# Scatters of token rows in pairs, gathered rows at another address, and the first expert's transposes spread between the last gate products

## The chip, the cores and the metric

One core of one Trainium2 chip runs the whole program. The metric is device time in microseconds (us), from the host's view of one execution; a profiled execution also has a span, from its first to its last instruction. Its engines work side by side and meet through semaphores: TensorE (PE, with PEld for its weight loads), VectorE (DVE), ScalarE (ACT), GpSimd (POOL) and SyncE (SP, which only starts transfers here).

## What is computed

Attention over q and k whose pairs count only where six sign bits of a projection agree, then a mixture of eight experts with two experts for each token, then a dense layer with a sigmoid gate. Cut from the reference:

```python
q_bits = (np.einsum('bhsd,dk->bhsk', q, proj) > 0)           # 2 x 8 heads x 768 x 64
mask = q_bucket[:, :, :, None] == k_bucket[:, :, None, :]
scores = np.where(mask, scale * q @ k.T, -1e9)
x = softmax(scores) @ v                                       # 1536 tokens x 512
noisy_logits = x @ w_gate + np.log1p(np.exp(x @ w_noise)) * noise
top2, top2_w = ...                                            # two experts of eight, softmax of the two
for e in range(8):
    out[mask] += top2_w * (np.maximum(x[mask] @ w1[e], 0) @ w2[e])
h = out @ w_in
return (h / (1 + np.exp(-1.702 * h))) @ w_out
```

## The kernel before

The 1536 tokens are four blocks `bq` of 384 (batch and half of the sequence), each of three row blocks of 128. The attention stage is one loop over `g` from -3 to 95 (L660 and on). A step holds the scores of one head's 128 queries against 768 keys two steps ahead (`a_score(g + 2)`, PE L320), their row maximum and the two scalars that the exponential wants (`a_soft`, DVE L332 to L334, tile `sm`), the transposes of the exponentials of step `g` (`a_trans`, PE L360, six of 128x128, whose copies out of PSUM go to ACT L289 or DVE L295), the exponential itself (ACT L343), every second step the product with the values (`a_av`, PE L370), and then the extra jobs that a table written by hand (`sched`) gives to that step. Tile then keeps the program's order on each engine; nothing is reordered.

Among the extra jobs are the hash and the operands of the heads to come (`a_hash`, PE L185; `a_hb`, DVE L200; `a_split` and `a_sub`, whose last part is a POOL subtraction, L219), gate products (`a_xt`, L410, with the DVE lines L403 to L417), routing (`r_do`), loads and splits of expert weights (`w_load`; `w_conv`, POOL L912), and the scatters. `r_scatter(bq, i)` sends row block `i` of `bq` to its two experts' row lists in HBM: two indirect DMAs issued by POOL (L513), each of 128 rows of 2 KB, and before each a one-element memset of a tile `spacer` (L512). On POOL they stand in trains: (0,0) and (0,1) are four scatters, (0,2) is two, bq 1 is six, bq 2 six, and bq 3 six in the expert stage.

After the loop comes the handover to the experts. The last two gate products `a_xt(15, 1)` and `a_xt(15, 2)` run; `f_tr` turns the first expert's rows (loaded as `xrow0`, three row blocks, 320 rows) by four PE transposes a block (L818) into `xeh`, copied by ACT (L819), with the remainders `xel` by a DVE subtraction (L820). PSUM banks of pool `ps_s` take two blocks and of `ps_p` one. Then the first expert's product (`f_s1`, PE L1048, 320 columns), the routing of bq 3 between its parts, and its rank products (PE L480) that need the table M (DVE L472).

At the other end, before the dense layer, `p_gather(t)` fetches each token's two expert results `yg` by indirect DMAs on POOL (L1268); `p_comb` weighs and adds them (ACT, DVE L1281 into `x`), and PE transposes the sum (L1295). The pool for this stage (`p_pools`) is laid over memory of the expert stage, in order of first use: `yg` comes first and lies where `xol` lay, which DVE L919 reads for its last split.

Of the kernel before, what the change touches and what calls it, by code (L numbers as in the profile page):

```python
# [9 lines left out]
F32 = mybir.dt.float32  # L10
# [4 lines left out]
AF = mybir.ActivationFunctionType  # L15
ALU = mybir.AluOpType
# [6 lines left out]
DM = 512  # L23
# [7 lines left out]
CAPA = 320  # L31
# [9 lines left out]
class Kernel:  # L41
# [282 lines left out]
    def a_soft(self, g):  # L324
        nc = self.nc
        u, s, n, qh, j, c = self.dec(g)
        ps = self.S.pop(g)
        if s == 0:
            self.RS[u] = self.rsum[u % 4]
        mx = self.t(self.ap, [128, 1], F32, "mx", 4)  # L330
        sm = self.t(self.ap, [128, 2], F32, "sm", 4)
        nc.vector.tensor_reduce(mx, ps[:, :, :HALF], axis=AX.XY, op=ALU.max, negate=True)  # L332
        nc.vector.tensor_scalar(sm[:, 0:1], mx, BIG / 2, None, op0=ALU.is_lt)
        nc.vector.tensor_scalar(sm[:, 1:2], mx, BIG / 2, mx, op0=ALU.is_lt, op1=ALU.mult)  # L334
        self.sm[g] = (sm, ps)
        self.use(dve=1.15)

    def a_exp(self, g):
# [170 lines left out]
    def r_scatter(self, bq, i):  # L509
        nc = self.nc  # L510
        for k in range(2):
            nc.gpsimd.memset(self.spacer, 0.0)  # L512
            st = nc.gpsimd.indirect_dma_start(  # L513
                out=self.xs, out_offset=bass.IndirectOffsetOnAxis(ap=self.slot[:, bq * 3 + i, k:k + 1], axis=0),
                in_=self.XR[bq][:, i, :], in_offset=None)
            for o in self.scat:
                self.tc.declare_no_dep(st.ins, o.ins, reason="every token has its own slot")
            self.scat.append(st)
# [15 lines left out]
    def attention(self):  # L534
# [3 lines left out]
        nc = self.nc  # L538
# [8 lines left out]
        for g, *f in (  # L547
# [158 lines left out]
            (56, self.w_load, 5),  # L706
            (56, self.r_do, 1, "soft"),
            (57, self.r_do, 1, "noisy", "top"),
            (57, self.r_scatter, 0, 1),
            (58, self.r_do, 1, "index"),  # L710
            (58, self.r_do, 0, "weights"),
            (59, self.w_conv, 4),
            (59, self.a_hash, 6),
# [19 lines left out]
            (67, self.r_scatter, 1, 0),  # L733
            (68, self.a_loadv, 6),
            (68, self.a_hash, 7),
            (69, self.r_scatter, 1, 1),
            (70, self.r_scatter, 1, 2),
            (70, self.a_hb, 7, 0),
            (70, self.a_uv, 7),
            (70, self.a_split, 7, 0, 0),  # L740
# [5 lines left out]
            (72, self.a_sub, 7, 1, 0, "p"),  # L746
            (73, self.a_xt, 11),
            (73, self.w_load, 6),
            (73, self.a_split, 7, 1, 1),
            (73, self.a_sub, 7, 1, 1, "p"),  # L750
            (75, self.w_load, 7),
# [31 lines left out]
            self.la, self.ld = max(self.la, 2.1 * g), max(self.ld, 2.1 * g)  # L783
        self.attn = False
        self.a_av(15, 2)
        self.a_xt(15, 1)
        self.a_xt(15, 2, True)
        self.f_tr()
        self.r_stage(3, 0, 3)
        self.r_do(3, "soft")  # L790
        self.f_s1(0)
# [15 lines left out]
            self.nc.sync.dma_start(t[:, i, :], x[i * 128:(i + 1) * 128, :])  # L807
        self.xrow[0] = t

    def f_tr(self):  # L810

        nc = self.nc
        xh, xl = self.xT[0] = self.x_tiles(0)
        for i, (o, w) in enumerate(self.tiles(0)):
            pt = self.t(self.ps_p, [128, 512], F32, "p") if i == 2 else self.t(self.ps_s, [128, 2, 512], F32, "s")[:, 0, :]
            pt = pt.rearrange("p (d n) -> p d n", d=4)
            for d in range(4):
                nc.tensor.transpose(pt[:, d, :], self.xrow[0][:, i, d * 128:(d + 1) * 128], self.ident)  # L818
            nc.scalar.activation(xh[:, :, o:o + w], pt[:, :, :w], AF.Copy)  # L819
            nc.vector.tensor_tensor(xl[:, :, o:o + w], pt[:, :, :w], xh[:, :, o:o + w].bitcast(F32), op=ALU.subtract)  # L820

    def f_s1(self, f):
        nc = self.nc
        ps = self.t(self.ps_s, [128, 2, 512], F32, "s")[:, 0, :CAPA]
        self.m_mm1(0, f, ps)
        if f >= 3:
            self.m_h(0, f, ps)
            return
        hh, hl = self.hT[0]
        h = self.t(self.ap, [128, CAPA], F32, "P", 3)  # L830
        nc.scalar.activation(h, ps, AF.Relu)
        nc.scalar.activation(hh[:, f, :], h, AF.Copy)
        nc.gpsimd.tensor_tensor(hl[:, f, :], h, hh[:, f, :].bitcast(F32), op=ALU.subtract)
# [421 lines left out]
    def p_pools(self, ctx):  # L1255
        self.pp = self.pool("mlp", ctx=ctx, side="right")
        self.ps_g = self.pool("ps_g", 2, PSUM, ctx=ctx)
        self.ps_o = self.pool("ps_o", 4, PSUM, ctx=ctx)
        self.ps_u = self.pool("ps_u", 2, PSUM, ctx=ctx)
        self.maxload = NU + 16  # L1260
        self.x2T, self.gT, self.op, self.yg, self.x2 = {}, {}, {}, {}, {}

    def p_gather(self, t):
        nc = self.nc
        ys = []
        for k in range(2):
            y = self.t(self.pp, [128, DM], F32, f"yg{k}", 2)
            st = nc.gpsimd.indirect_dma_start(  # L1268
                out=y, out_offset=None, in_=self.ys,
                in_offset=bass.IndirectOffsetOnAxis(ap=self.ysl[:, t, k:k + 1], axis=0))  # L1270
            ys.append(y)
            if t < 6:
                self.early.append(st)
        self.yg[t] = ys
# [331 lines left out]
```

## Time and profile before

| | us |
|---|---|
| median of 3 runs | 863.45 (861.52, 863.50, 863.45) |
| the profiled execution | 861.88 |
| its span | 860.2 |
| PE busy in the span | 838.9 (98%) |
| DVE, ACT, POOL busy | 524.7, 434.4, 222.8 |
| mean granted TensorE clock | 0.994 |

The profile gives for each engine its busy time, for each instruction when it began, how long it ran and how long its engine stood idle ahead of it (with what ended that). A row in square brackets below names an engine's idle time and the instruction that ended it. The granted clock is 1.00 at TensorE's full 2.4 GHz and 0.50 at its lower level of 1.2 GHz.

### The profile page before, as it was taken

Reading aid. Unit: us, or ns where it says so; the run is one execution under the profiler, and the core shown is the slowest. Engines: PE = TensorE matmul, PEld = TensorE weight load, DVE = VectorE, ACT = ScalarE, POOL = GpSimd, SP = SyncE. Lnnn points to the kernel's source line nnn. Section 1 sums busy time; section 2 is a strip of 40 time slices with the busy share of each in tenths; the row PEclk is TensorE's granted clock in tenths of the full one; section 3 lists DMA queues with packets and bytes.
Section 4 is the critical chain, followed back from the end, with each engine's and each line's share of the span. In section 5 each row is a group of like instructions: output and inputs, shape, how many; then the busy total and the mean of one; then the engine's idle time right before and its main releaser. Section 6 shows DMA issues by size and latency. Waiting matters only on the chain.

```text
span 860.2 us, 15512 instructions
## 1 busy us (share of the span) xinstructions
PE 838.9 (98%) x6104; PEld 775.6 (90%) x6104; DVE 524.7 (61%) x1068; ACT 434.4 (51%) x772; POOL 222.8 (26%) x235
## 2 busy tenths in 40 slices
PE   8999999889989999999999999998999999999997
PEld 6888888769979999999999999988899998989897
DVE  7787878667764698989889898747622121312120
ACT  6887988757763544454545353556623131414140
POOL 4531746474024000000000000007614151504040
PEclk9999999999999999999999999999999999999999
DMA  7646845441135577877879686738301010010000
GB/s 253 215 151 217 237 139 162 148 135 45 38 112 208 199 250 245 293 238 258 280 247 291 207 288 207 239 111 317 124 26 50 25 42 33 27 49 2 25 1 28
DMA packets 49854, 132.47 MB, mean 154 GB/s; under 512 B 6256, under 2 KB 8496, under 8 KB 49776
## 3 DMA queue, kind: packets, MB, share of 16 engines
q1 hardware_dynamic: 41280, 109.38, 38.5%
q0 software_dynamic: 6960, 20.37, 7.7%
q10 hardware_dynamic: 1536, 1.67, 0.6%
q8 instruction: 50, 0.82, 0.4%
q14 instruction: 28, 0.23, 0.1%
HBM read 92.23 MB, written 35.39 MB: 148 GB/s over the span
## 4 chain that ended last, share of the span: by engine, by line
PE 93%; DMA 2%; DVE 2%; another core or an unknown queue 1%; issue 1%; ACT 1%; ACTq 0%; POOL 0%; DVEq 0%; POOLq 0%; SPq 0%
PE g L1318 15%; PE h L1048 15%; PE s L320 8%; PE av L370 8%; PE p L360 7%; PE y L1070 5%; PE y L1072 5%; PE y L1071 5%; PE o L1365 4%; PE o L1363 4%; PE o L1364 4%; PE s L1048 2%; PE t L1089 2%; DMA rawk<-in_kT 1%; PE t L1025 1%; PE m L410 1%
## 5 line engine op out<-in xcount | busy, mean ns | idle before, releaser
L332 DVE TENSOR_REDUCE mx<-s 128x1 f32<-128x768 f32 x96 | 91.6, 954 | 31.8 <-PE s L320 25.3
L1327 POOL TENSOR_TENSOR gl<-sg,gh 128x512 fp32r<-128x512 f32 x48 | 66.1, 1376 | 157.6 <-ACT gh L1326 157.6
L343 ACT ACTIVATE P<-s,sm 128x768 f32<-128x768 f32 x96 | 95.3, 993 | 22.3 <-DVE sm L334 20.2
L1268 POOL DMA_INDIRECT yg<-ys,cst x24 | 25.5, 1062 | 303.2 <-DVE wl L919 296.8
L320 PE MATMUL s<-v,u 76*128 76x384 f32 (+1 forms) x384 | 93.3, 364 | 0.4 <-ACT P L343 0.2
L1323 DVE TENSOR_TENSOR sg<-g,sg 128x512 f32<-128x512 f32 x48 | 33.2, 692 | 93.6 <-ACT sg L1322 91.7
L360 PE MATMUL p<-cst,P 128*128 128x128 f32 x576 | 80.3, 275 | 9.2 <-ACT hh L289 4.5
L360 PEld LDWEIGHTS p<-cst,P 128*128 128x128 f32 x576 | 68.8, 141 | 15.0 <-ACT hh L289 5.8
L320 PEld LDWEIGHTS s<-v,u 76*128 76x128 f32 (+1 forms) x384 | 63.4, 191 | 13.7 <-issue 9.0
L1053 ACT ACTIVATE hh<-h 128x416 fp32r<-128x416 f32 x56 | 29.1, 519 | 72.9 <-PE h L1048 72.4
L1070 PE MATMUL y<-hh,wh 128*128 128x416 f32 (+1 forms) x144 | 51.1, 355 | 0.0
L1322 ACT ACTIVATE sg<-g 128x512 f32<-128x512 f32 x48 | 28.7, 599 | 42.2 <-PE g L1318 38.0
L1072 PE MATMUL y<-hh,wl 128*128 128x416 f32 (+1 forms) x144 | 49.8, 346 | 0.0
L1071 PE MATMUL y<-hl,wh 128*128 128x416 f32 (+1 forms) x144 | 49.8, 346 | 0.0
L1326 ACT ACTIVATE gh<-sg 128x512 fp32r<-128x512 f32 x48 | 30.3, 631 | 31.7 <-DVE sg L1323 30.9
L1054 DVE SCALAR_TENSOR_TENSOR hl<-h,hh 128x416 fp32r<-128x416 f32 x56 | 32.9, 588 | 14.4 <-ACT hh L1053 14.2
L289 ACT ACTIVATE hh<-p 128x384 f32<-128x384 f32 x71 | 31.7, 487 | 17.1 <-PE p L360 7.8
L1318 PE MATMUL g<-bth,wh 128*128 128x256 f32 x144 | 39.9, 277 | 0.0
L1318 PE MATMUL g<-x2h,wh 128*128 128x256 f32 x144 | 39.9, 278 | 0.0
L1318 PE MATMUL g<-btl,wh 128*128 128x256 f32 x144 | 39.8, 276 | 0.0
L1318 PE MATMUL g<-bth,wl 128*128 128x256 f32 x144 | 39.8, 276 | 0.0
L1318 PE MATMUL g<-x2h,wl 128*128 128x256 f32 x144 | 39.7, 277 | 0.0
(328 smaller groups left out, 2489.4 us busy)
## 6 DMA issues: line engine op xcount, KB each, us to landing
ws<-in_w SPq DMA_DIRECT2D x40, 512.0 KB, 5.8
d_in<-in_w SPq DMA_DIRECT2D x32, 512.0 KB, 5.3
bth<-in_w SPq DMA_DIRECT2D x16, 512.0 KB, 4.6
btl<-in_w SPq DMA_DIRECT2D x16, 512.0 KB, 4.9
wd<-d_o SPq DMA_DIRECT2D x32, 256.0 KB, 3.8
xs<-xeh SPq DMA_DIRECT2D x13, 512.0 KB, 6.0
rawq<-in_qT SPq DMA_DIRECT2D x14, 384.0 KB, 5.3
rawk<-in_kT SPq DMA_DIRECT2D x14, 384.0 KB, 4.7
```

Source lines behind the costliest of these rows:

```text
L320: nc.tensor.matmul(ps[:, hf, :HALF], l[:kk, q0:q0 + 128], r[:kk, hf * HALF:(hf + 1) * HALF], start=st, stop=not st)
L332: nc.vector.tensor_reduce(mx, ps[:, :, :HALF], axis=AX.XY, op=ALU.max, negate=True)
L343: nc.scalar.activation(P, ps[:, :, :HALF], AF.Exp, bias=sm[:, 1:2], scale=sm[:, 0:1], accum_out=self.RS[u][:, c, j, 0:1])
L360: nc.tensor.transpose(ps[:, kb, :], P[:, hf, kb * 128:(kb + 1) * 128], self.ident)
L370: nc.tensor.matmul(self.pa[64 * j:64 * j + 64, c * 128:(c + 1) * 128], self.vt[n][:, kb, 64 * j:64 * j + 64], PT[:, j, kb, :], start=(kb = ...
L1048: nc.tensor.matmul(ps, self.units[8 * e + d][w][:, fs], y[:, d, :n], start=(i == 0), stop=(i == 11))
L1070: nc.tensor.matmul(ps, wh[:, ds_], hh[:, f, :], start=(f == 0), stop=False)
L1071: nc.tensor.matmul(ps, wh[:, ds_], hl[:, f, :], start=False, stop=False)
L1072: nc.tensor.matmul(ps, wl[:, ds_], hh[:, f, :], start=False, stop=(f == 7))
L1318: nc.tensor.matmul(ps[:, x, :], self.units[NU + 4 * (f // 8) + d][w][:, fs], y[:, d, :], start=(i == 0), stop=(i == 11))
L1327: nc.gpsimd.tensor_tensor(gl[:, fo, :], g, gh[:, fo, :].bitcast(F32), op=ALU.subtract)
L1363: nc.tensor.matmul(ps, gh[:, f, o], wh[:, ws], start=(f == 0), stop=False)
```

## The change

Three edits:

1. The scatters of bq 0 and 1. Ahead of the first of each pair, the spacer is no longer a memset but a POOL copy from the newest `sm` tile, kept in `self.smt`: POOL waits until DVE has written the scalars of score `g + 2`. The second keeps its memset. In the table, (0,1) moves from step 57 to 58, (1,1) from 69 to 70, and (1,2) from 70 to 73. (0,0), (0,2) and (1,0) keep their steps.
2. `f_tr` becomes `f_hi` (a block's PE transposes and ACT copy) and `f_lo` (its DVE remainder). The blocks stand before `a_xt(15, 1)` and between it and `a_xt(15, 2)`; their banks are now one of `ps_s`, one of `ps_p` and the product's own `pa`; the first product of the expert goes to the bank of the gate products (`mt`).
3. `p_pools` reserves four buffers (`sg` and `x2`, two each) ahead of all others, so that `yg` comes 8 KB a partition further on, over `yT` and `yrow`.

```diff
@@ -333,6 +333,7 @@
         nc.vector.tensor_scalar(sm[:, 0:1], mx, BIG / 2, None, op0=ALU.is_lt)
         nc.vector.tensor_scalar(sm[:, 1:2], mx, BIG / 2, mx, op0=ALU.is_lt, op1=ALU.mult)
         self.sm[g] = (sm, ps)
+        self.smt = sm
         self.use(dve=1.15)
 
     def a_exp(self, g):
@@ -509,7 +510,10 @@
     def r_scatter(self, bq, i):
         nc = self.nc
         for k in range(2):
-            nc.gpsimd.memset(self.spacer, 0.0)
+            if bq < 2 and k == 0:
+                nc.gpsimd.tensor_copy(self.spacer, self.smt[0:1, 0:1])
+            else:
+                nc.gpsimd.memset(self.spacer, 0.0)
             st = nc.gpsimd.indirect_dma_start(
                 out=self.xs, out_offset=bass.IndirectOffsetOnAxis(ap=self.slot[:, bq * 3 + i, k:k + 1], axis=0),
                 in_=self.XR[bq][:, i, :], in_offset=None)
@@ -706,8 +710,8 @@
             (56, self.w_load, 5),
             (56, self.r_do, 1, "soft"),
             (57, self.r_do, 1, "noisy", "top"),
-            (57, self.r_scatter, 0, 1),
             (58, self.r_do, 1, "index"),
+            (58, self.r_scatter, 0, 1),
             (58, self.r_do, 0, "weights"),
             (59, self.w_conv, 4),
             (59, self.a_hash, 6),
@@ -733,8 +737,7 @@
             (67, self.r_scatter, 1, 0),
             (68, self.a_loadv, 6),
             (68, self.a_hash, 7),
-            (69, self.r_scatter, 1, 1),
-            (70, self.r_scatter, 1, 2),
+            (70, self.r_scatter, 1, 1),
             (70, self.a_hb, 7, 0),
             (70, self.a_uv, 7),
             (70, self.a_split, 7, 0, 0),
@@ -746,6 +749,7 @@
             (72, self.a_sub, 7, 1, 0, "p"),
             (73, self.a_xt, 11),
             (73, self.w_load, 6),
+            (73, self.r_scatter, 1, 2),
             (73, self.a_split, 7, 1, 1),
             (73, self.a_sub, 7, 1, 1, "p"),
             (75, self.w_load, 7),
@@ -783,9 +787,13 @@
             self.la, self.ld = max(self.la, 2.1 * g), max(self.ld, 2.1 * g)
         self.attn = False
         self.a_av(15, 2)
+        self.f_hi(0)
         self.a_xt(15, 1)
+        self.f_hi(1)
+        self.f_hi(2)
+        for i in range(3):
+            self.f_lo(i)
         self.a_xt(15, 2, True)
-        self.f_tr()
         self.r_stage(3, 0, 3)
         self.r_do(3, "soft")
         self.f_s1(0)
@@ -807,21 +815,28 @@
             self.nc.sync.dma_start(t[:, i, :], x[i * 128:(i + 1) * 128, :])
         self.xrow[0] = t
 
-    def f_tr(self):
-
-        nc = self.nc
-        xh, xl = self.xT[0] = self.x_tiles(0)
-        for i, (o, w) in enumerate(self.tiles(0)):
-            pt = self.t(self.ps_p, [128, 512], F32, "p") if i == 2 else self.t(self.ps_s, [128, 2, 512], F32, "s")[:, 0, :]
-            pt = pt.rearrange("p (d n) -> p d n", d=4)
-            for d in range(4):
-                nc.tensor.transpose(pt[:, d, :], self.xrow[0][:, i, d * 128:(d + 1) * 128], self.ident)
-            nc.scalar.activation(xh[:, :, o:o + w], pt[:, :, :w], AF.Copy)
-            nc.vector.tensor_tensor(xl[:, :, o:o + w], pt[:, :, :w], xh[:, :, o:o + w].bitcast(F32), op=ALU.subtract)
+    def f_hi(self, i):
+        nc = self.nc
+        if i == 0:
+            self.xT[0] = self.x_tiles(0)
+            self.xps = []
+        o, w = self.tiles(0)[i]
+        pt = (self.t(self.ps_s, [128, 2, 512], F32, "s")[:, 0, :] if i == 0 else self.t(self.ps_p, [128, 512], F32, "p") if i == 1
+              else self.pa)
+        pt = pt.rearrange("p (d n) -> p d n", d=4)
+        for d in range(4):
+            nc.tensor.transpose(pt[:, d, :], self.xrow[0][:, i, d * 128:(d + 1) * 128], self.ident)
+        nc.scalar.activation(self.xT[0][0][:, :, o:o + w], pt[:, :, :w], AF.Copy)
+        self.xps.append(pt)
+
+    def f_lo(self, i):
+        o, w = self.tiles(0)[i]
+        xh, xl = self.xT[0]
+        self.nc.vector.tensor_tensor(xl[:, :, o:o + w], self.xps[i][:, :, :w], xh[:, :, o:o + w].bitcast(F32), op=ALU.subtract)
 
     def f_s1(self, f):
         nc = self.nc
-        ps = self.t(self.ps_s, [128, 2, 512], F32, "s")[:, 0, :CAPA]
+        ps = self.t(self.ps_s, [128, 2, 512], F32, "s")[:, 0, :CAPA] if f else self.mt([128, CAPA])
         self.m_mm1(0, f, ps)
         if f >= 3:
             self.m_h(0, f, ps)
@@ -1259,6 +1274,10 @@
         self.ps_u = self.pool("ps_u", 2, PSUM, ctx=ctx)
         self.maxload = NU + 16
         self.x2T, self.gT, self.op, self.yg, self.x2 = {}, {}, {}, {}, {}
+        for _ in range(2):
+            self.t(self.pp, [128, 2, self.CH], F32, "sg", 2)
+        for _ in range(2):
+            self.t(self.pp, [128, DM], F32, "x2", 2)
 
     def p_gather(self, t):
         nc = self.nc
```

On POOL, from the last weight split ahead of bq 1's scatters to their end (`wl` is that split; `xel` holds bq 1's rows; `u_8`, `v_8` are the last head's operands). Before:

```order
L912 TENSOR_TENSOR wl_2751<-ws_2359,wh_2750 128x1024
L512 MEMSET spacer_138 1x1
L513 DMA xs<-xel_761,slot_137 15360x512
...
L170 DMA u_8_2906<-u_8_2905 64x768
...
L219 TENSOR_TENSOR v_8_2910<-rawk_8_2268,v_8_2909 64x768
L219 TENSOR_TENSOR u_8_2907<-rawq_8_2270,u_8_2907 64x768
L219 TENSOR_TENSOR v_8_2912<-rawk_8_2272,v_8_2911 64x768
```

After:

```order
L927 TENSOR_TENSOR wl_2751<-ws_2359,wh_2750 128x1024
L514 COPY spacer_138<-sm_2760 1x1
L517 DMA xs<-xel_761,slot_137 15360x512
...
L514 COPY spacer_138<-sm_2867 1x1
...
L170 DMA u_8_2902<-u_8_2901 64x768
...
L219 TENSOR_TENSOR u_8_2903<-rawq_8_2270,u_8_2903 64x768
L514 COPY spacer_138<-sm_2986 1x1
...
L219 TENSOR_TENSOR v_8_2908<-rawk_8_2272,v_8_2907 64x768
```

Where six scatters stood in a row behind the weight split, there are two pairs now, the second behind a copy of its own, and the third pair stands between the last two subtractions of the head's operands.

On PE, from the last product with the values to the first expert's first product (`xrow` are the expert's rows, `xu` the attention rows of the last two gate products). Before:

```order
L370 MATMUL av_96<-hl_3695,v_3173 64x128 x12
L410 MATMUL m_3753<-cst_124,xu_3718 128x160
L410 MATMUL p_3761<-cst_124,xu_3751 128x160
L818 MATMUL s_3771<-cst_124,xrow_1_3624 128x128 x4
L818 MATMUL s_3778<-cst_124,xrow_1_3624 128x128 x4
L818 MATMUL p_3785<-cst_124,xrow_1_3624 128x128 x4
L1048 MATMUL s_3806<-xeh_3769,wh_1412 128x320
```

After:

```order
L371 MATMUL av_96<-hl_3695,v_3173 64x128 x12
L828 MATMUL s_3755<-cst_124,xrow_1_3624 128x128 x4
L411 MATMUL m_3761<-cst_124,xu_3718 128x160
L828 MATMUL p_3769<-cst_124,xrow_1_3624 128x128 x4
L828 MATMUL av_96<-cst_124,xrow_1_3624 128x128 x4
L411 MATMUL p_3783<-cst_124,xu_3751 128x160
L1063 MATMUL m_3805<-xeh_3753,wh_1412 128x320
```

The first block's transposes now stand ahead of both gate products, the others between them. On DVE the three `xel` subtractions accordingly stand ahead of the last gate product's lines instead of behind them.

## Rows read from the trace of the kernel before

**Rows 1.** Waits of PE over the whole span: us in total, times, longest.

```profile
PE p L360 <- ACT hh L289: 4.5, 3, 2.5
PE u L1295 <- DVE x L1281: 2.3, 2, 1.5
```

**Rows 2.** Windows: length; busy PE, PEld, DVE, ACT, POOL; granted clock, DMA share, GB/s.

```profile
124.78:134.36 9.58, 9.58 (x105) 8.12 (x104) 8.42 (x30) 7.01 (x17) 0.00 (x0) 1.00 0.16 59
149.36:163.84 14.48, 11.96 (x106) 9.65 (x105) 8.98 (x38) 8.23 (x19) 4.28 (x7) 0.88 0.43 167
168.54:178.19 9.65, 9.65 (x96) 8.79 (x95) 7.76 (x27) 9.11 (x20) 9.07 (x12) 1.00 0.58 154
183.38:200.13 16.75, 12.49 (x105) 9.80 (x104) 8.47 (x19) 6.79 (x13) 10.53 (x19) 0.80 0.46 146
241.00:257.00 16.00, 12.79 (x127) 10.75 (x126) 9.72 (x34) 9.25 (x21) 6.33 (x11) 1.00 0.41 149
192.00:195.00 3.00, 2.48 (x14) 1.75 (x16) 2.01 (x5) 2.13 (x4) 0.00 (x0) 0.50 0.23 87
```

**Rows 3.** POOL's scatters in the timeline: start, us, instruction, idle before it.

```profile
149.45 1.09 POOL L513 DMA_INDIRECT xs<-xr,slot  x1 [0.18 <-DVE xeh L417]
153.41 0.97 POOL L513 DMA_INDIRECT xs<-xr,slot  x1 [0.22 <-issue]
...
172.16 1.05 POOL L513 DMA_INDIRECT xs<-xr,slot  x1 [0.17 <-POOL spacer L512]
...
184.23 1.02 POOL L513 DMA_INDIRECT xs<-xel,slot  x1 [0.16 <-issue]
...
190.66 0.97 POOL L513 DMA_INDIRECT xs<-xel,slot  x1 [0.21 <-issue]
```

**Rows 4.** PE and DVE at the first stall of each of the two trains, timeline.

```profile
153.73 0.96 DVE L332 TENSOR_REDUCE mx<-s 128x1 f32<-128x768 f32 x1 [2.21 <-PE s L320]
155.67 0.93 PE L360 MATMUL p<-cst,P 128*128 128x128 f32 x6 [2.52 <-ACT hh L289]
188.46 0.68 DVE L200 TENSOR_SCALAR hb<-p,hdr 128x384 fp32r<-128x384 f32 x1 [2.94 <-PE p L360]
189.19 0.55 PE L360 MATMUL p<-cst,P 128*128 128x128 f32 x3 [2.23 <-issue]
```

**Rows 5.** POOL's last subtractions and PE's scores behind them, timeline.

```profile
196.54 0.56 POOL L170 DMA_DIRECT2D u<-u  x1 [4.91 <-ACT u L169]
207.11 1.82 POOL L219 TENSOR_TENSOR v<-rawk,v 64x768 fp32r<-64x768 f32 x1
211.18 0.97 PE L320 MATMUL s<-v,u 128*128 128x384 f32 x4
```

**Rows 6.** The handover to the first expert, timeline of ACT, PE and DVE.

```profile
259.54 0.28 ACT L289 ACTIVATE xu<-av 128x128 f32<-128x128 f32 x1 [1.61 <-PE av L370]
260.88 1.08 ACT L819 ACTIVATE xeh<-s 128x512 fp32r<-128x512 f32 x2 [1.06 <-PE s L818]
261.86 0.39 ACT L819 ACTIVATE xeh<-p 128x256 fp32r<-128x256 f32 x1
262.95 0.38 PE L1048 MATMUL s<-xeh,wh 128*128 128x320 f32 x1 [1.23 <-DVE xel L820]
266.98 0.21 DVE L472 TENSOR_REDUCE M<-oh 128x24 bf16<-128x48 f32 x1
268.29 0.18 PE L480 MATMUL m<-M,tri 128*128 128x8 bf16 x1
```

**Rows 7.** Around the first gather, timeline of ACT's queue, DVE and POOL.

```profile
573.28 0.33 ACTq L1102 DMA_DIRECT2D ys<-xel  x1
575.88 1.22 DVE L919 TENSOR_TENSOR wl<-xol,wh 128x1024 fp32r<-128x1024 f32 x1
577.89 1.02 POOL L1268 DMA_INDIRECT yg<-ys,cst  x1 [296.50 <-DVE wl L919]
```

**Rows 8.** DMA issues from 565 to 592: KB each, median us to landing.

```profile
ys<-xeh ACTq DMA_DIRECT2D x2, 128.0 KB, 1.8
```

## Prediction

> **What bounds the kernel now.** I read the shares of busy time first: TensorE (PE) is busy in 838.9 of 860.2 us, so the program takes PE's work plus PE's few gaps. The waits of PE come next: they are short, and those that the change can touch are the ones behind the copies of the transposes, 4.5 us in three [rows 1], the 2.3 us in front of the dense stage [rows 1], and one at the handover to the experts [rows 6]. Then the busy time by window, which shows what a gap costs besides itself. Two rounds of the attention loop (four steps, with one hash) take 9.58 us when nothing disturbs them; PE fills all of it at a granted clock of 1.00 [rows 2]. The same four steps around the four scatters of 149.45 to 154.38 take 14.48, and around the six scatters of 184.23 to 191.63 they take 16.75 [rows 2, 3]. In the first, PE is idle 14.48 - 11.96 = 2.52, and busy 11.96 - 9.58 = 2.38 longer for the same work; in the second, idle 4.26 and busy 2.91 longer [rows 2]. The longer part is the clock: behind the second train three microseconds ran at 0.50, the 1.2 GHz level, after PE had stood [rows 2]. So the trains cost 4.90 and 7.17 us, half as idle time and half as slower matmuls.
>
> Why do the engines stand? The first row of DVE behind each train's start is told to wait for PE's product, though that product was long done, and the PE row is told to wait for an ACT copy or for nothing at all [rows 4]: three engines that work at different things stop together, and go on when the train is near its end. That speaks for notices between engines that come late while a long train of scattered packets goes out, not for a missing operand. What makes a train harmless is shown by the lone pair (0,2): two scatters at 172.16, and its window takes 9.65 at a clock of 1.00, with a DMA share (0.58) higher than in either train [rows 2, 3]. Nearly the same work as the 9.58, so the pair cost 0.07. In the four-scatter train the first 2.1 us, the time of about the first pair, were free too: DVE's idle time of 2.21 ended at 153.73, so it began at 151.52 [rows 3, 4].
>
> **The change part by part.**
>
> *Scatters.* The change leaves every scatter (POOL's work is the same) and breaks the four into (0,0) and (0,1), the six into (1,0), (1,1) and (1,2), each pair behind scalars of a later score. The copy replaces a memset of a single element; I price both at nothing, since POOL is not on the path and one more wait on it matters only for what is queued there. If each pair behaves like the lone one, the trains give back 4.90 + 7.17 = 12.07, less five times 0.07 = 0.35. From the other side, each train's first stall could stay whole: 2.52 and 2.23 [rows 4], 4.75 in all, because the two pairs that stand first, (0,0) and (1,0), keep their places beside a weight load and right behind a long POOL split. I take 1.5 in between, 0.3 for (0,0) and 1.2 for (1,0): in the first train the first pair is free by the row above, but in the second DVE stood from 188.46 - 2.94 = 185.52, while the third scatter, at a spacing of (190.66 - 184.23) / 5 = 1.29, began only at 186.81 [rows 3, 4]; about half of the first stall of 2.23 can belong to the pair. So **-12.07 + 1.5**.
>
> *What is queued behind POOL's new waits.* At (1,1) POOL waits for score 72's scalars, and behind it stand the operand transfers and subtractions of the last head, which PE's score 79 needs; (1,2) now stands ahead of the very last subtraction. Before, that one ended at 208.93 and PE used it in the second half of the score at 211.18, so 211.6: 2.7 of slack, against a pair's 172.16 to 174.51 with its memset, 2.6 [rows 3, 5]. But with both trains gone PE comes sooner too, so I count both from the start of score 72. PE: seven steps by 9.58 / 4 = 16.8, and 0.4 to the second half, 17.2 [rows 2]. POOL: score 0.97, maximum 0.96, two small ones 0.3, so 2.2 [rows 4, 5]; pair 2.6; five transfers by 0.56 = 2.8; three subtractions by 1.82 = 5.5 with one more transfer between, 0.56; pair 2.6; the last subtraction 1.8 [rows 3, 5]; in all 18.1. PE waits 0.9 there, once: **+0.9**, between 0 (if ACT's splits, on which that head waited 4.91 before [rows 5], come early and PE loses time elsewhere) and 2.65, a whole pair. (0,1) also waits for a score's scalars, but only a weight split with much slack is behind it; at (1,0) and (1,2) POOL arrives later than the scalars.
>
> *Handover.* Before the change, the first expert product begins at 262.95 after 1.23 of idle time; it wants all of `xeh` [rows 6]. ACT had finished the attention copy at 259.82, then stood 1.06 until the transposes behind the two gate products were done [rows 6]. With block 0's transposes right behind the product with the values, and the others while the gate products run, ACT's three copies (1.08 + 0.39 = 1.47) follow at 259.82 without a hole, to 261.3, and the product starts at about 261.4: 1.55 sooner. DVE's remainders are needed by the ninth product only, 1.2 later, and come by then. What is next: the rank products need M, which DVE ends at 267.19 while PE came at 268.29 [rows 6]. DVE does the same work in front of M in another order and gains perhaps 0.3; PE, 1.55 sooner, comes at 266.74 and waits some 0.4. So **-1.1**, between 0 (if DVE is the chain throughout) and -1.55. The stores and loads on SP behind it keep their order.
>
> *Gathers.* The first gather starts 0.79 after DVE's last split of `xol` (575.88 + 1.22 = 577.10), the memory that `yg` takes [rows 7]. At the new address nothing of DVE's stands ahead of it, only the stores of `ys`, the last of them issued at 573.28 and landing in 1.8 [rows 7, 8]: 575.1, and 0.8 on gives 575.9, 2.0 sooner. PE waits for the sums 2.3 in two waits [rows 1], so nearly all of it is taken: **-2.0**, between -1.3 (DVE's splits now stand between the gathered rows and their sums) and the whole -2.3. Loads behind the gathers on POOL come sooner by the same and have slack.
>
> *The sum* is 861.88 - 12.07 + 1.5 + 0.9 - 1.1 - 2.0 = **849.1**. The third train, bq 2's six scatters, is untouched and keeps its 3.21 of idle time (16.00 - 12.79, at a clock of 1.00) [rows 2]. The profiled execution lies 1.6 below the median of the runs; on the median's footing the sum is 850.7. I say **850.0**.
>
> **The rivals.**
>
> *A: the first pairs still stall.* Where the weight load runs beside, and POOL's split ends right there, (0,0) and (1,0) keep 2.52 and 2.23. For it: DVE's idle time in the second train began before the third scatter. Against it: the lone pair ran beside more transfers than either train. Instead of 1.5 it costs 4.75: 849.1 + 3.25 = 852.4. Chance 0.25.
>
> *B: it isn't the length of a train.* The stalls come from something else that is there at 150 and 185 (the expert weight load, the routing that starts there), and breaking the trains only moves or keeps them. Then only handover and gathers gain: 861.88 - 1.1 - 2.0 + 0.9 = 859.7. For it: one lone pair is thin evidence. Against it: idle time of all engines at once is found only at trains [rows 2, 4]. Chance 0.10. The Trainium skill, page "SBUF — State Buffer", section "Who interferes with whom", says that DMA never contends with a compute engine and that PE and ACT never wait on anyone; by it the scatters would not be what stops PE, and the time would be this rival's. The trace disagrees as far as it goes: PE stands 2.52 and 4.26 us in just these windows.
>
> *C: slower, by starts.* What costs is not the length but the start of a train, when POOL begins to write scattered packets while others run; then five starts instead of two, each like the first train, cost 5 x 4.90 = 24.5 in place of 12.07: 861.88 + 24.5 - 12.07 - 3.1 + 0.9 = 872.1. It decides from p with 5 p > 12.07 + 3.1 - 0.9 + 2.6, p = 3.4 us a pair. The lone pair with its 0.07 speaks against it, and only that. Chance 0.05.
>
> **How the numbers follow.** My forecast has 0.57, A 0.25, B 0.10, C 0.05, and 0.03 is left for what I haven't seen. The range takes in the forecast with its bounds and A: low, the sum with all terms at their good ends (the pairs at 0.35, no wait for the subtraction, the whole handover, the whole wait at the gathers), 849.1 - 1.15 - 0.9 - 0.45 - 0.3 = 846.3, so 846; high, A with 1.75 more for the late subtraction and 0.7 for the gathers and 1.6 for the median's footing, 856.5, so 857. B and C lie outside. A measurement of this kernel can tell about 0.3%, 2.6 us, from no change. Faster by more: the forecast, A, and the better part of the rest, 0.86; within: B nearly whole, 0.09; slower: C, 0.05.
>
> **What would show it.** Right: in the waits of PE the row of `p` behind ACT's copies loses most of its 4.5; windows of four steps around each pair take 9.6 to 10 at a clock of 1.00; POOL's copy of `sm` waits at (0,1) and (1,1); PE waits about 1 us for POOL's last subtraction ahead of one score; the first expert product starts some 1.5 us sooner after the last product with the values, and PE then waits shortly at the rank products; the first gather follows the last store by 2 to 3 us and PE's waits at L1295 shrink below 0.5; the train of bq 2 still has 3.2 of idle time. Wrong: a clock below 0.9 around pairs, or a new wait of PE for POOL of over 2.7 us, or idle time at the first pairs like that of rows 4.

## The result

The changed kernel takes 853.13 us against 862.58 for the kernel before, in runs made together: a ratio of 0.9897 (0.9883 to 0.9911), 9.45 us less. The forecast was 850.0 with 846 to 857 around it. The profiled executions are 851.73 against 861.88 (spans 849.9 and 860.2), 10.15 apart.

Most runs made together (a session) lie within 0.3% of their median and a few up to 0.5% above it, but sessions differ by more: in three of them, the one above included, the kernel before takes 860.3 to 862.6 us, in two it takes 846.5 and 846.8, and one and the same chip was seen with 860.3 and with 846.8. I call them stalling and quiet sessions. Ratios compare runs of one session only.

The waits of PE of the changed kernel (us in total, times, longest), to be held against [rows 1]:

```profile
PE m L411 <- issue: 2.9, 1, 2.9
PE u L1314 <- DVE x L1300: 1.4, 2, 0.8
...
PE s L320 <- POOL spacer L516: 1.2, 1, 1.2
PE p L361 <- DVE hb L200: 1.2, 2, 0.9
```

The transposes' wait behind ACT's copies, 4.5 us before, is nearly gone (0.3 in one wait). What is left at the trains is the 2.9 of the third, which the change doesn't touch, and 1.2 for `hb`, of which 0.28 stand behind (0,1) and 0.92 behind (1,0):

```profile
159.26 0.55 PE L361 MATMUL p<-cst,P 128*128 128x128 f32 x3 [0.28 <-DVE hb L200]
183.79 0.55 PE L361 MATMUL p<-cst,P 128*128 128x128 f32 x3 [0.92 <-DVE hb L200]
```

The wait for POOL is the new one, at score 79. The windows answer to [rows 2]; the first line is the place of (0,0) and (0,1), the second the lone pair, the third (1,0) and (1,1), the last the start of the third train:

```profile
148.84:159.74 10.90, 10.62 (x105) 8.19 (x104) 8.91 (x38) 7.57 (x19) 4.42 (x8) 1.00 0.58 225
164.45:174.10 9.65, 9.65 (x95) 8.80 (x94) 7.77 (x27) 9.25 (x20) 9.14 (x12) 1.00 0.57 160
179.30:190.01 10.71, 9.79 (x105) 8.11 (x105) 8.44 (x20) 6.86 (x13) 5.75 (x11) 1.00 0.35 126
231.00:247.00 16.00, 12.56 (x114) 10.76 (x112) 9.80 (x31) 8.82 (x19) 6.26 (x11) 1.00 0.42 147
```

The same four steps took 14.48 and 16.75 before, with granted clocks of 0.88 and 0.80; now they take 10.90 and 10.71 at 1.00. The clock's part of the loss is gone with the idle time. The forecast had 9.6 to 10 for such windows. POOL in the timeline, as [rows 3, 5]: the copy waits for DVE's scalars, a pair runs, and the last subtraction begins only when the third pair is out, after which PE's score goes on:

```profile
155.25 0.18 POOL L514 COPY spacer<-sm 1x1 f32<-1x1 f32 x1 [3.83 <-DVE sm L334]
...
186.43 0.18 POOL L514 COPY spacer<-sm 1x1 f32<-1x1 f32 x1 [3.87 <-DVE sm L334]
...
198.61 1.05 POOL L517 DMA_INDIRECT xs<-xel,slot  x1 [0.18 <-POOL spacer L514]
...
200.98 1.82 POOL L219 TENSOR_TENSOR v<-rawk,v 64x768 fp32r<-64x768 f32 x1
...
202.85 0.63 PE L320 MATMUL s<-v,u 76*128 76x384 f32 x2 [1.20 <-POOL spacer L516]
```

At the handover, as [rows 6], the three copies no longer come in one piece behind the gate products, and the rank products follow PE's products without a wait, since M is done at 257.90 + 0.21 = 258.11:

```profile
251.12 0.28 ACT L289 ACTIVATE xu<-av 128x128 f32<-128x128 f32 x1 [1.61 <-PE av L371]
251.70 0.60 ACT L829 ACTIVATE xeh<-s 128x512 fp32r<-128x512 f32 x1 [0.31 <-PE s L828]
252.41 0.60 ACT L829 ACTIVATE xeh<-p 128x512 fp32r<-128x512 f32 x1
252.91 0.38 ACT L829 ACTIVATE xeh<-av 128x256 fp32r<-128x256 f32 x1
253.34 0.41 PE L1063 MATMUL m<-xeh,wh 128*128 128x320 f32 x1 [0.25 <-ACT xeh L829]
257.90 0.21 DVE L473 TENSOR_REDUCE M<-oh 128x24 bf16<-128x48 f32 x1
258.71 0.18 PE L481 MATMUL m<-M,tri 128*128 128x8 bf16 x1
```

And at the gathers, as [rows 7]:

```profile
566.29 1.22 DVE L934 TENSOR_TENSOR wl<-xol,wh 128x1024 fp32r<-128x1024 f32 x1
566.64 1.77 POOL L1287 DMA_INDIRECT yg<-ys,cst  x1 [294.85 <-ACT xrow L1149]
568.72 0.97 POOL L1287 DMA_INDIRECT yg<-ys,cst  x1 [0.30 <-issue]
```

The first gather no longer waits for DVE's split of `xol`: it runs beside it, and takes 1.77 us instead of 1.02.

### The profile page after: what moved, and what is told of

It is laid out like the page before. It is cut to its first block, busy times and chain, and to the rows that moved or that the text cites. A ratio compares the mean times of both kernels' runs of the same rounds, so it can differ in the third digit from the quotient of the medians.

```text
span 849.9 us, 15514 instructions
## 1 busy us (share of the span) xinstructions
PE 834.7 (98%) x6104; PEld 772.6 (91%) x6104; DVE 524.0 (62%) x1068; ACT 434.2 (51%) x772; POOL 224.0 (26%) x235
## 4 chain that ended last, share of the span: by engine, by line
PE 92%; DVE 3%; DMA 1%; POOL 1%; ACT 1%; another core or an unknown queue 1%; issue 1%; ACTq 0%; DVEq 0%; POOLq 0%
PE g L1337 16%; PE h L1063 15%; PE s L320 8%; PE av L371 7%; PE p L361 7%; PE y L1085 6%; PE y L1087 6%; PE y L1086 6%; PE o L1384 4%; PE o L1382 4%; PE o L1383 4%; PE t L1104 2%; PE s L1063 1%; PE t L1040 1%; PE m L411 1%; DVE mx L332 1%
## 5 line engine op out<-in xcount | busy, mean ns | idle before, releaser
L1085 PE MATMUL y<-hh,wxh 128*128 128x416 f32 (+1 forms) x112 | 39.7, 354 | 0.0
```

What stands on the lines that cost most here:

```text
L1085: nc.tensor.matmul(ps, wh[:, ds_], hh[:, f, :], start=(f == 0), stop=False)
```

## The experiments

**One edit at a time (stalling session, kernel before 860.49).** The kernel before with the scatters' edit alone, which is the diff without `f_hi`, `f_lo` and the four reserved buffers:

> The kernel before with the first edit alone (pairs behind the copy, new steps). If the account from the two traces holds, the scatters give 3.6 at the first train and 6.0 at the second and take 1.5 back at the last subtraction: 8.1 us of the 9.4 of the whole change, so 854 to 855.5 against a before of 862.6. Rival: the three edits need each other, since the whole change makes every later transfer earlier; then this alone gives clearly less than 7.

Measured 854.93, a ratio of 0.9933 (0.9917 to 0.9950), 5.6 us less. That is 2.5 short of the expected gain. The places themselves did what was expected: four-step windows of 10.82 and 10.63, and a wait of 1.2 for POOL's subtraction.

```profile
152.51:163.33 10.82, 10.54 (x106) 8.21 (x105) 8.93 (x38) 7.58 (x19) 4.43 (x8) 1.00 0.58 226
182.89:193.52 10.63, 9.80 (x105) 8.11 (x105) 8.45 (x20) 6.85 (x13) 5.75 (x11) 1.00 0.37 127
```

The profiled execution of this kernel lost 3.1 in its first 18 us, of which 10 ran at clocks of 0.50 and 0.53, which says how much one execution can differ. I leave the 2.5 open: either the three edits give more together, or a part of the 9.45 belongs to its own set of runs, since the changed kernel was not measured beside these runs.

The changed kernel with the scatters put back:

> The changed kernel with the scatters as before: the spread transposes and the other address of the gathered rows only. By the traces 0.9 at the handover and 1.1 at the gathers, 2.0 us in all, 860.6 against 862.6; both trains keep 4.9 and 7.2. The prediction's own terms would give 3.1. In the trace the first gather should last about 1.8 us again, because a DVE split with two operands in SBUF runs beside it.

Measured 858.60, 0.9979 (0.9966 to 0.9992), 1.9 less, as expected from the traces, and not the 3.1 of the prediction's terms. Both trains keep their windows (14.08 and 16.86), and the first gather lasts 1.59, again beside the split.

**Is it the wait, or the place in the table? (same session)** The copy gives way to the memset; all places stay new.

```diff
-            if bq < 2 and k == 0:
-                nc.gpsimd.tensor_copy(self.spacer, self.smt[0:1, 0:1])
-            else:
-                nc.gpsimd.memset(self.spacer, 0.0)
+            nc.gpsimd.memset(self.spacer, 0.0)
```

> The changed kernel with the memset in place of the copy, so that nothing spaces the pairs: on POOL (0,0) and (0,1) follow each other again as four scatters, (1,0) and (1,1) as four, and (1,2) is a pair behind two subtractions. If the wait is what helps: four-step windows of 14 to 14.5 us at the first place (as before) and 13.5 to 14.5 at the second, 859 to 861.5 in all. Rival: the place in the table is what helps (fewer scatters in the step of the routing); then the time stays at 853.

Measured 857.25, less than the 859 to 861.5 expected and far from the 853 of the rival. The two windows of this kernel, at (0,0) with (0,1), and at (1,0) with (1,1), each four scatters in a row now:

```profile
149.02:162.91 13.89, 12.06 (x106) 9.45 (x105) 9.01 (x38) 8.35 (x19) 4.29 (x7) 0.88 0.47 181
182.45:196.07 13.62, 11.37 (x106) 9.24 (x105) 8.39 (x19) 6.68 (x13) 7.75 (x15) 0.87 0.46 136
```

Nothing but the gap between the pairs differs from the changed kernel, and the stalls and the lower clock are back: 13.89 and 13.62 against 10.90 and 10.71. The new steps alone leave four in a row at both places, since POOL has no other work between these pairs. Six in a row cost more than four (16.75 before), and two little. In a stalling session the length of an unbroken train is the cause, and the wait is the means. Why a train stops the engines stays open: that notices between them come late, as the prediction reads its rows, was not tried by any run.

**The floor under the pairs (same session).**

```diff
     def r_scatter(self, bq, i):
         nc = self.nc
+        if bq < 2:
+            return
```

> The changed kernel without any scatter of bq 0 and bq 1 (half the experts' rows are left out): the floor under the pairs. If what is left around (0,0) and (0,1) (10.90 us against an undisturbed 9.58) and around (1,0) and (1,1) (10.71) is the scatters', both windows fall to 9.6 here. If it is the routing and the hash beside them on DVE and ACT, the first window stays near 10.9. And without the pair ahead of it the last subtraction should be in time, so no wait of PE for POOL.

This kernel leaves out half of the experts' rows. The windows at the two places of pairs, and between them one that nobody had expected:

```profile
149.19:159.28 10.09, 10.09 (x106) 8.29 (x105) 8.71 (x38) 7.70 (x19) 0.00 (x0) 1.00 0.35 135
163.98:174.00 10.02, 8.55 (x85) 7.34 (x84) 9.00 (x17) 6.59 (x14) 9.27 (x9) 1.00 0.40 103
174.00:178.00 4.00, 2.10 (x9) 2.00 (x10) 3.50 (x11) 2.86 (x7) 0.00 (x0) 0.79 0.00 0
184.25:193.83 9.58, 9.58 (x106) 8.13 (x105) 8.47 (x19) 6.78 (x13) 1.58 (x4) 1.00 0.20 60
```

At the first place the four steps take 10.09 without any scatter: some 0.5 over the undisturbed 9.58 belongs to what else runs there, not to scatters; that it is the routing is argued, not shown. At the second they take 9.58. So both guesses were half right: the pairs cost 0.8 and 1.1 there. The new stall at 168 to 178, in which no scatter runs, is told of at the end; with it this kernel is no faster (853.23, a single run) than the changed one.

**Place against length (quiet session, kernel before 846.84).** (0,1) goes to the lone pair's step.

```diff
-            (58, self.r_scatter, 0, 1),
...
+            (61, self.r_scatter, 0, 1),
             (61, self.r_scatter, 0, 2),
```

> The changed kernel with (0,1) moved from step 58 to step 61, right ahead of (0,2): a train of four at the place where the lone pair cost nothing, with no weight load just issued and no routing table beside it; the first place keeps (0,0) alone. If the length of a train counts, the four steps at that place grow from 9.65 by 3 to 4.5 us (four in a row cost 3.8 and 4.0 at the two other places in the run without the copy), and the first place falls from 10.90 to about 10.5; 855 to 857 in all. If the place counts (rival B), the four steps stay below 10.5 and the time at 853 or less.

Measured 847.68, and the changed kernel beside it 846.76. Neither theory was tried by it: among these runs no train stalls at all. The same kernel once more:

> The kernel with four scatters in a row at the lone pair's place again, since the first time it ran in a session in which no train of any kind stalled PE. Where the kernel before takes 860: if length counts, the four steps there grow from 9.65 by 3 to 4.5 us and the time is 855 to 857; if the place counts, they stay below 10.5 and the time is 853 or less.

Again a quiet session: 847.18 with 846.51 for the kernel before. Four in a row at the lone pair's place stay untried where trains stall.

**The changed kernel in the quiet session.**

> The changed kernel once more, on the same chip as the three runs beside it: 853 against 861 to 862.5 for the kernel before.

The expectation failed outright: 846.76 against 846.84, a ratio of 1.000 (0.999 to 1.001). Its windows at the first pairs, at the second, and at the third train:

```profile
148.95:159.28 10.33, 10.30 (x105) 8.26 (x105) 8.91 (x38) 7.62 (x19) 4.41 (x8) 1.00 0.62 239
178.83:188.41 9.58, 9.58 (x105) 8.13 (x104) 8.54 (x20) 6.73 (x13) 5.74 (x11) 1.00 0.40 141
229.40:245.40 16.00, 16.00 (x166) 14.07 (x164) 11.97 (x43) 11.04 (x25) 6.29 (x11) 1.00 0.42 149
```

The last line decides. It is the same program, the same six scatters in a row at the same place, the same DMA share (0.42) and bytes (149 GB/s against 147) as in the last window of the result; yet PE is busy in all of its 16.00 us instead of 12.56. The pairs cost little or nothing here either: 10.33 is 0.2 over the 10.09 without scatters, 9.58 is the undisturbed time. What a train costs is not the kernel's alone. The third train shows it in every profile: from the rank products ahead of it (PE L481, or L480 before) to the start of the last product with the values (L371, or L370) PE takes 14.81 us in each of the six quiet ones, and 18.0 to 20.9 in the eight stalling ones.

**The kernel before, with a profile of its own (stalling session, 860.33).**

> The kernel before, unchanged, with a profile of its own, because the chip decides: on two chips it took 861.7 and 860.5 us, on the third 846.8, and there the changed kernel took the same 846.8. If the trains are the whole of the difference between chips, this run shows one of two pictures. Near 861: windows of 14.1 to 14.5 us at the four scatters and 16.8 at the six, as before. Near 847: both windows at 9.6 to 10.2 and no wait of PE behind the copies of the transposes, though the scatters' packets are the same. Rival: the difference of 14 us lies elsewhere (first loads, the clock in the expert stage).

The first picture came, 860.59, on the chip that had been quiet, so the chip does not decide:

```profile
149.13:163.20 14.07, 12.09 (x105) 9.59 (x105) 8.99 (x38) 8.35 (x19) 4.29 (x7) 0.88 0.45 173
182.75:199.41 16.66, 12.49 (x105) 9.80 (x104) 8.47 (x19) 6.79 (x13) 10.52 (x19) 0.80 0.46 147
```

Against the quiet floors of 10.33 and 9.58 that is 3.7 and 7.1; the third train, between the same two products, takes 18.27, which is 3.5 more than 14.81. The sum, 14.3, is about the 13.5 to 13.8 that separates the sessions of the kernel before. So the trains account for about the whole of it. That is put together from two kernels: a profile of the kernel before in a quiet session is missing.

**The late subtraction (quiet session, 846.84).**

```diff
-            (73, self.r_scatter, 1, 2),
             (73, self.a_split, 7, 1, 1),
             (73, self.a_sub, 7, 1, 1, "p"),
+            (73, self.r_scatter, 1, 2),
```

> The changed kernel with the pair (1,2) behind POOL's last subtraction instead of ahead of it. Theory: PE's wait for that subtraction (1.20, and 1.46 by the positions of the scores) goes away, and the pair is as cheap there as elsewhere: 1.2 to 1.5 us faster than the changed kernel beside it. Rival: the pair then runs beside the next head's last scores and stalls them, and the gain is below 0.5.

Measured 845.15, a ratio of 0.9982 (0.9973 to 0.9992) to the kernel before, 1.6 under the changed kernel beside it. PE's wait for POOL is gone, and four steps with a gate product take 8.77 where the changed kernel took 10.20. This term doesn't depend on the session.

**The third train.** Pairs in steps 89, 90 and 91, and the expert's rows loaded in 92.

```diff
-            if bq < 2 and k == 0:
+            if bq < 3 and k == 0:
...
-            (89, self.r_scatter, 2, 1),
-            (89, self.r_scatter, 2, 2),
+            (90, self.r_scatter, 2, 1),
+            (91, self.r_scatter, 2, 2),
...
-            (91, self.f_load,),
+            (92, self.f_load,),
```

> The changed kernel with the third train, bq 2's six scatters, in pairs too: (2,0) in step 89, (2,1) in 90, (2,2) in 91, each behind the copy of the newest scalars, and the load of the expert's rows in step 92. If length and spacing are the cause, PE's 2.9 us of waiting there shrink below 1 and the time falls by 2 to 3 us. What could eat it: the expert's rows come later and PE waits for them at the handover; and with a pair in every step the gaps are shorter (2.2 us a step against 2.6 a pair), so that the pairs may still act as a train.

In the quiet session it gives 846.95: the 2 to 3 us didn't come, and where trains don't stall they can't. With the edit of the late subtraction, in a stalling session:

> The changed kernel with the pair (1,2) behind the last subtraction and bq 2's scatters in pairs too. Where trains stall (the kernel before near 861): 1.4 from the subtraction and 2.5 to 4 from the third train against the changed kernel's 853, so 848 to 849.5. Where they don't (near 847): 845.2, as with the first of the two edits alone, since the other then changes nothing.

Measured 849.35 against 860.33, a ratio of 0.9871 (0.9851 to 0.9892). The changed kernel had 0.9897 in another stalling session; the intervals overlap, and the 1.5 us between the two gains is no more than the subtraction alone gives. Between the two products named above the third train still takes 18.05, against 18.76 in the changed kernel and 14.81 when quiet. That is 0.7 of 3.9, and less than the spread among the seven stalling profiles in which the train is whole (18.01 to 20.85), so a gain there is not shown. POOL gives a reason; the second and third copy wait for nothing, and the three pairs are one train again:

```profile
234.22 0.97 POOL L517 DMA_INDIRECT xs<-xeh,slot  x1 [0.21 <-issue]
235.20 0.18 POOL L514 COPY spacer<-sm 1x1 f32<-1x1 f32 x1
235.53 0.98 POOL L517 DMA_INDIRECT xs<-xeh,slot  x1 [0.16 <-issue]
```

So I set the pairs two steps apart, (2,1) in step 91 and (2,2) in step 93, the rows loaded behind it, again with the edit of the late subtraction:

> The changed kernel with (1,2) behind the last subtraction and bq 2's pairs two steps apart: (2,0) at once in step 89, (2,1) behind the scalars of step 91, (2,2) behind those of step 93, the expert's rows loaded right after. With pairs in every step (the run before) the third train still cost 3.4 of 3.8. If a gap is what a pair needs, the train now costs 1 or less, 2.5 to 3 us faster than that run, 846.5 to 847.5 where the kernel before takes 860; against it, the rows come some 1.5 us late and PE waits at the handover for them, then 848. In a session without stalls: 845 to 847, with that wait alone.

It met a quiet session (846.51) and cost 848.99, 1.0031 (1.0017 to 1.0045). The price is plain, and twice the 1.5 that I had put on it:

```profile
247.36 0.66 PE L828 MATMUL s<-cst,xrow 128*128 128x128 f32 x4 [3.13 <-DMA xrow<-xs]
```

PE waits 3.1 us for the expert's rows, and behind that wait it runs at a clock of 0.50 from 249.5 to 252.2. What the gaps give back in a stalling session stays open.

## Why the prediction was right, and where it was not

The time lies in the range and the sign is right; the account holds less well than the total. The range was wide enough for the forecast and for rival A both.

- **Trains.** The mechanism holds: the stalls of 2.52 and 2.23 are gone where the trains are broken. "Each pair behaves like the lone one" holds in part. PE is idle 0.92 behind (1,0), where I had put 1.2; behind (0,0), where I had put 0.3, it is not idle at all, and 0.28 follow (0,1). And the 0.07 of the lone pair compares windows of different work (96 and 105 matmuls): the row shows that PE was never idle there, not what the pair cost. The first term was over-sized too. I took 9.58 as the floor of both places; it is 9.58 at the second and 10.1 to 10.3 at the first, where more runs beside the loop. So the four-scatter train cost 4.2 to 4.4 rather than 4.90, and 3.58 came back at that place; at the other 6.04 came back, where 7.17 - 1.2 was expected.
- **Late subtraction.** The mechanism was right, the size was +0.9 forecast and +1.4 to 1.6 measured.
- **Handover.** The forecast was -1.1. The first expert product begins 253.34 - 251.12 = 2.22 after ACT's last attention copy instead of 3.41, so 1.2 sooner, and not 1.55, since ACT waits 0.31 for transposes ahead of its first copy and 0.11 ahead of the second (252.41 - 251.70 - 0.60). The wait at the rank products that I subtracted didn't come: from the same copy they are 7.59 away instead of 8.75. Two errors that cancel.
- **Gathers.** The forecast was -2.0; PE's waits fell from 2.3 to 1.4, not below 0.5. Two steps failed. One is "0.8 on": by it the first gather would have started 2.0 sooner as measured from DVE's split, and it started 1.7 sooner (0.35 behind the split's start instead of 2.01); the trace names an ACT instruction (L1149) that ended 0.10 before, and whether that or the stores held it is open. The other is a length that the sum took as unchanged: the gather lasted 0.75 longer beside the split, so that the second came only 0.9 sooner (2.43 behind the split's start instead of 3.34, by the row of the kernel before):

```profile
579.22 0.98 POOL L1268 DMA_INDIRECT yg<-ys,cst  x1 [0.30 <-issue]
```

Together: -3.6 - 6.0 + 1.4 - 1.2 - 0.9 = -10.3, against the 12.77 of the sum.

Rival A gave 852.4 on the footing of the profiled execution, where the forecast had 849.1 and 851.73 came, so the total is nearer to A. But A's mechanism is wrong: the first pairs don't keep their stalls of 2.52 and 2.23. A total near a rival's number is no proof of it, and that ours lies in the range is in part luck, since the missing 2.5 is the sum of three terms that were each off by 0.5 to 1.1. Rival B, that length isn't the cause, falls where trains stall, by the run with memsets. What the Trainium skill says on the page that B cites ("SBUF — State Buffer", section "Who interferes with whom"), that DMA never contends with a compute engine and that PE and ACT never wait on anyone, doesn't carry over to these trains: that run differs from the changed kernel in the gap between transfers alone, and PE stands 1.83 and 2.25 us in its two windows (13.89 - 12.06 and 13.62 - 11.37). In a quiet session its forecast of the scatters (nothing to gain) is what happened, for a reason that no rival named. Rival C is out: two pairs together cost 0.8 and 1.1, and one would have to cost 3.4.

What I could not have read from one trace is that the stalls themselves come and go. In a quiet session the change is worth 0.1 +- 0.8 us. By the terms above, the late subtraction takes some 1.4 of the 2.1 that handover and gathers give; a profile of the kernel before in a quiet session, which could show it, is missing. What tells the sessions apart is open; the trace shows the same transfers in both.

## What to carry to other kernels

Break trains of indirect scatters into pairs with a real wait between them where engines meet often; a change of order that leaves four in a row on the issuing queue leaves the stall. Here 4.5 us from the end of a pair to the start of the next were enough (151.42 to 155.92), and some 0.3 were not shown to help; what lies between was not tried where trains stall. Before a piece of work is moved on a queue, list what stands behind it there and when it is needed: here 1.4 us went that way, and moving the pair one instruction later got them back in the quiet session; in a stalling one the wait was gone as well, in a kernel with another edit besides. And before a stall is priced from one profile, see it in a second session.

## What was not expected of the hardware

**A stall that depends on the session.** Trains of scatters stop PE, DVE and ACT and cost 3 to 7 us each in some sessions, and not at all in others, with equal packets and equal bytes. The changed kernel was profiled with and without them, and one chip ran the kernel before in a session of each kind.

**POOL's arithmetic holds up small DVE work.** Without the lone pair, POOL's subtractions came earlier and met the routing of bq 0. In the run without scatters (timeline of DVE, POOL and PE):

```profile
167.89 1.81 POOL L219 TENSOR_TENSOR v<-rawk,v 64x768 fp32r<-64x768 f32 x1
169.77 1.82 POOL L219 TENSOR_TENSOR u<-rawq,u 64x768 fp32r<-64x768 f32 x1
171.67 1.80 POOL L219 TENSOR_TENSOR v<-rawk,v 64x768 fp32r<-64x768 f32 x1
...
167.90 1.82 DVE L497 TENSOR_TENSOR macc<-rw,macc 128x8 bf16<-128x8 f32 x1
170.07 1.55 DVE L504 TENSOR_SCALAR rv<-rv 128x3 f32<-128x3 f32 x1 [0.27 <-ACT rv L503]
171.87 1.63 DVE L506 TENSOR_TENSOR cst<-rv,cst 128x3 f32<-128x3 f32 x1
...
175.90 1.32 PE L320 MATMUL s<-v,u 128*128 128x384 f32 x4 [2.86 <-ACT P L344]
```

Three DVE operations on a few columns, which take 0.17 each in the changed kernel, end with the POOL subtraction that runs beside them. The maximum behind them comes late, ACT's exponential with it, and PE stands 2.86, after which the clock is 0.79 on the mean. The Trainium skill, page "SBUF — State Buffer", section "Who interferes with whom", describes such a lock: DVE and GpSimd share a pair of ports, and the second to come waits for the whole of the first's instruction. The rows agree for the two-operand forms; L504 has one operand and was held as well.

**A gather's issue beside a DVE split.** The first gather takes 1.77 beside a DVE subtraction of two SBUF operands. In all eleven profiles with the new address the two run side by side and it takes 1.59 to 1.79; in the three with the old one it starts behind the split and takes 1.02 or 1.03. The same page says that a DVE instruction with two inputs in SBUF contends with a GpSimd instruction that reads SBUF, and this would be a case of it. But it also infers that such a DVE instruction does not hold up the making of a DMA's descriptors, and by that the gather would keep its length; the rows go against it. No run changed the split alone, so the rows show only that the two go together.
